# Chunked attention ahead of a two-layer MLP: scores in 64x32 parts and values in 64x64 parts of the PE array

## The chip, the cores and the metric

The kernel runs on one core of one Trainium2 chip. The metric is the device time of one execution in microseconds (us), lower is better. The kernel before takes 1089.06 us, the median of three runs (1088.07 to 1089.83).

## What is computed

Attention over chunks of 32 tokens (4 batches, 8 heads, 768 tokens, head size 64), then two MLP layers. Each chunk sees 8 memory keys, 16 tokens to its left, itself and 8 tokens to its right, 64 keys in all (fewer at the ends of the sequence).

```python
q_c = q[:, :, c_start:c_end]                       # 32 queries
k_full = np.concatenate([mem_k, k_ctx], axis=2)    # 8 + up to 56 keys
v_full = np.concatenate([mem_v, v_ctx], axis=2)
scores = scale * np.matmul(q_c, k_full.transpose(0, 1, 3, 2))
a = np.exp(scores - np.max(scores, axis=-1, keepdims=True))
a = a / (np.sum(a, axis=-1, keepdims=True) + 1e-09)
out[:, :, c_start:c_end] = np.matmul(a, v_full)
...
x = attn_out.transpose(0, 2, 1, 3).reshape(3072, 512)
h = x @ w_in                       # 512 -> 2048
y = softplus(h) @ w_out            # 2048 -> 512
# second layer: the same shapes, with PReLU (alpha per column) for softplus
```

## The kernel before

**Attention** is cut into 24 tiles t of 128 tokens (`QT`); a tile has four chunks and 8 heads in 4 pairs (`NPAIR`). For one tile, in this order:

- SP loads Q in two halves (`load_q`, 64 partitions each), K (`load_k`) and V in six pieces (`load_v`). Loads go through one in-order queue; each waits until the eighth before it has landed. POOL copies the 8 memory keys to both ends of K's runs (`a_mem`, two copies).
- PE computes the scores (`a_scores`). For tiles 0 to 7 that is 32 matmuls on parts of 64 rows by 32 columns of the array: the two heads of a pair (e = 0, 1) lie on the two halves of the rows, and head e of chunk c writes the 32 PSUM partitions c*64 + e*32, so that four different parts are used in turn. For tiles 8 to 23 it is 16 matmuls on 128 rows by 64 columns, with queries that are zero in the other head's places (`q_late`, zeroed once by `others`). The result fills one PSUM bank.
- DVE takes the maximum (`a_max`) and subtracts it (`a_shift`), ACT takes the exponential, DVE sums and inverts, and DVE (POOL for tiles 4 to 7) scales. For tiles 0 to 3 DVE only scales the maximum (`a_bias`), and ACT subtracts and exponentiates in eight pieces.
- PE transposes (`a_transpose`, 4 matmuls), and ACT copies the result to `pt` in four pieces (`a_turned`), into corners of a block form whose other corners are zero (`no_corners`, once).
- PE multiplies by V (`a_values`: 16 matmuls on 128 rows by 64 columns, with 64 columns streamed). ACT writes the high part of x (`a_high`), DVE the low part (`a_low`).

PSUM's eight banks are four for accumulators (`ps_acc`; the first four tiles' scores use them too), two for `ps_h` and two for attention (`ps_a`), which scores, transposes and values take in turn.

**Layer 1** has 96 steps; step i multiplies 512 tokens (block b, four tiles) by one weight column block f. A step is two units of 12 matmuls each: `pe_h` (x times w_in, written `ps_hh` in the profile) and `pe_out` (activation times w_out, `ps_o`). Steps 0 to 3 are block 0 with f = 0 to 3, steps 4 to 7 block 1 with the same weights; so step 4 needs tiles 4 to 7. Each weight half comes as a raw load of 64-bit words (`raw`), which DVE converts with five operations (`word`), ACT rounds to a high part (`wsplit`), and DVE subtracts for a low part. Three raw buffers are in use at a time; the next raw load waits until DVE is done with the one three before. **Layer 2** (`ps_q`) follows.

**The order** of all of this is laid down by a planner (`Plan`, `schedule`): each piece has an engine, an assumed duration, a due time, things it must follow, and rooms that it takes and gives. The table `O` shifts due times by kind of piece. Every engine then runs its pieces strictly in that order, so an operation that waits for a DMA holds all that stands behind it on its engine. Where PE would idle in the first 90 us of the plan, matmuls on zeros fill in (`keep_busy`).

In the rows below all instructions have line L71, since a helper issues them; they are told apart by the names of their tiles: `ps_s` scores, `ps_t` transposes, `ps_x` values, `qk`, `qt`, `kt`, `v` the loaded inputs, `x` the attention's result, `g` the activation.

Of the kernel before, what the change touches and what calls it, by code (L numbers as in the profile page):

```python
# [185 lines left out]
def attention_mlp_mlp_kernel(ctx: ExitStack, tc, qk, v, w1, w2, consts, out):  # L186
# [129 lines left out]
    raw_q, q_t, k_t, v_t, st, s_room = {}, {}, {}, {}, {}, {}  # L316
    pt = [tpool.tile([P, NPAIR, 2, D], F32, tag=tag, name="pt") for tag in ("tb", "tl")]
    both = gpool.tile([P, 2, NPAIR, 2, D], F32, tag="g", name="pt2")
    pt2 = [both[:, u] for u in range(2)]

    def pt_of(t):
        return pt2 if t < TB and t % 2 else pt

    q_late = apool.tile([P, 2, 4 * NPAIR, CHUNK], F32, tag="qt", name="qt", bufs=1)

    def others(q, eng):
# [868 lines left out]
```

## Time and profile before

| | |
|---|---|
| median of three runs | 1089.06 us |
| profiled execution, its own time | 1092.29 us |
| its span (first to last instruction) | 1090.2 us |
| PE busy (matmul) | 97% of the span |
| DVE, ACT, POOL busy | 65%, 51%, 16% |
| mean granted TensorE clock | 0.995 of full speed |

The profile gives for each engine its instructions in order of time with the idle time just before them and what released it, and a chain of work that is followed back from the last instruction. The profiled execution's time is 2.1 us above its span and 3.2 us above the median.

### The profile page before, as it was taken

Reading aid. Unit: us, or ns where it says so; the run is one execution under the profiler, and the core shown is the slowest. Engines: PE = TensorE matmul, PEld = TensorE weight load, DVE = VectorE, ACT = ScalarE, POOL = GpSimd, SP = SyncE. Lnnn points to the kernel's source line nnn. Section 1 sums busy time; section 2 is a strip of 40 time slices with the busy share of each in tenths; the row PEclk is TensorE's granted clock in tenths of the full one; section 3 lists DMA queues with packets and bytes.
Section 4 is the critical chain, followed back from the end, with each engine's and each line's share of the span. In section 5 each row is a group of like instructions: output and inputs, shape, how many; then the busy total and the mean of one; then the engine's idle time right before and its main releaser. Section 6 shows DMA issues by size and latency. Waiting matters only on the chain.

```text
span 1090.2 us, 16860 instructions
## 1 busy us (share of the span) xinstructions
PE 1061.8 (97%) x6241; PEld 872.5 (80%) x6245; DVE 705.3 (65%) x1182; ACT 556.9 (51%) x988; POOL 173.0 (16%) x217
## 2 busy tenths in 40 slices
PE   5789999999999999999999999999999999999998
PEld 3568888878888888888888888888888888888886
DVE  5779978454554454464366256678766779566976
ACT  4564435455544554453244346664455755456643
POOL 1110112422322232224233400000000010000000
PEclk8999999999999999999999999999999999999999
DMA  8966674757554554554365484799875999856904
GB/s 216 203 178 190 192 188 109 180 159 178 152 156 148 167 174 125 184 156 136 106 203 189 161 300 137 274 286 323 199 284 174 322 298 261 242 217 256 373 1 77
DMA packets 173841, 214.56 MB, mean 197 GB/s; under 512 B 96064, under 2 KB 125888, under 8 KB 166848
## 3 DMA queue, kind: packets, MB, share of 16 engines
q1 hardware_dynamic: 169456, 196.59, 56.8%
q0 software_dynamic: 4032, 16.78, 8.2%
q8 instruction: 49, 0.80, 0.3%
q14 instruction: 32, 0.26, 0.1%
q10 hardware_dynamic: 272, 0.13, 0.0%
HBM read 154.74 MB, written 46.14 MB: 184 GB/s over the span
## 4 chain that ended last, share of the span: by engine, by line
PE 92%; DMA 4%; SPq 2%; DVE 2%; issue 0%; ACT 0%; POOL 0%; DVEq 0%; ACTq 0%
PE ps_q L71 42%; PE ps_hh L71 23%; PE ps_o L71 23%; SPq L71 2%; DMA raw<-in_w_dram 2%; PE ps_x L71 2%; PE ps_s L71 2%; DMA v<-in_v_dram 1%; PE ps_t L71 1%; DVE word L71 1%; DMA qk<-in_qk_dram 1%; DVE x L71 0%; DVE wsplit L71 0%; DVE g L71 0%; ACT pt L71 0%
## 5 line engine op out<-in xcount | busy, mean ns | idle before, releaser
L71 PE MATMUL ps_o<-g,wsplit 128*128 128x512 f32 x1152 | 281.2, 393 | 1.3 <-DVE g L71 1.3
L71 PE MATMUL ps_hh<-x,wsplit 128*128 128x512 f32 x1152 | 279.4, 391 | 2.9 <-ACT x L71 1.8
L71 PEld LDWEIGHTS ps_hh<-x,wsplit 128*128 128x128 f32 x1152 | 214.7, 188 | 48.6 <-ACT x L71 2.3
L71 PEld LDWEIGHTS ps_o<-g,wsplit 128*128 128x128 f32 x1152 | 215.8, 189 | 46.6 <-DVE g L71 1.6
L71 PE MATMUL ps_q<-xop,win 128*128 128x512 f32 x1008 | 229.1, 389 | 0.0
L71 PE MATMUL ps_q<-g,wout 128*128 128x512 f32 x1008 | 229.1, 389 | 0.0
L71 PEld LDWEIGHTS ps_q<-xop,win 128*128 128x128 f32 x1008 | 189.2, 188 | 39.3
L71 PEld LDWEIGHTS ps_q<-g,wout 128*128 128x128 f32 x1008 | 189.0, 188 | 39.6 <-DVE g L71 0.2
L71 DVE TENSOR_TENSOR g<-ta,g 128x512 fp32r<-128x512 f32 x96 | 70.4, 733 | 131.1 <-ACT g L71 130.6
L71 ACT CAST g<-gb 128x512 fp32r<-128x512 f32 x168 | 100.9, 622 | 91.1 <-PE ps_q L71 66.1
L71 DVE TENSOR_TENSOR g<-gb,g 128x512 fp32r<-128x512 f32 x168 | 114.2, 687 | 37.0 <-ACT g L71 35.1
L71 ACT CAST g<-ta 128x512 fp32r<-128x512 f32 x96 | 59.6, 621 | 113.9 <-PE ps_o L71 113.7
L71 ACT ACTIVATE ta<-ps_hh 128x512 f32<-128x512 f32 x96 | 57.4, 598 | 108.9 <-PE ps_hh L71 106.6
L71 DVE SCALAR_TENSOR_TENSOR word<-raw,word 128x512 int32<-128x512 int32 x128 | 93.0, 727 | 2.7
L71 ACT ACTIVATE tp<-gb 128x512 f32<-128x512 f32 x48 | 30.4, 633 | 91.5 <-DVE gb L71 91.5
L71 POOL TENSOR_TENSOR wst<-wsum,wst 128x512 fp32r<-128x512 f32 x32 | 42.8, 1338 | 146.9 <-ACT wst L71 146.9
L71 DVE TENSOR_SCALAR word<-raw 128x512 int32<-128x512 int32 x64 | 29.6, 463 | 51.2 <-DMA raw<-in_w_dram 31.7
L71 DVE SCALAR_TENSOR_TENSOR gb<-gb,tp 128x512 f32<-128x512 f32 x48 | 33.2, 692 | 44.0 <-ACT tp L71 44.0
L71 DVE TENSOR_SCALAR word<-word 128x512 f32<-128x512 f32 (+1 forms) x128 | 56.6, 447 | 1.9
L71 ACT ACT_TABLE_LOAD x38 | 48.8, 1283 | 12.0 <-DVE nm L71 11.3
L71 POOL TENSOR_TENSOR wst<-word,wst 128x512 fp32r<-128x512 f32 (+1 forms) x32 | 35.2, 1100 | 119.2 <-ACT wst L71 119.2
L71 POOL DMA_DIRECT2D gb<-gb x12 | 10.3, 862 | 262.7 <-DVE g L71 169.8
(82 smaller groups left out, 879.3 us busy)
## 6 DMA issues: line engine op xcount, KB each, us to landing
wout<-out_ops SPq DMA_DIRECT2D x42, 1024.0 KB
raw<-in_w_dram SPq DMA_DIRECT2D x64, 512.0 KB
win<-in_ops SPq DMA_DIRECT2D x24, 1024.0 KB
win<-in_ops SPq DMA_DIRECT2D x24, 768.0 KB
out_ops<-wst SPq DMA_DIRECT2D x56, 256.0 KB
in_ops<-wst SPq DMA_DIRECT2D x24, 512.0 KB
gb<-gb POOLq DMA_DIRECT2D x12, 1024.0 KB, 13.7
v<-in_v_dram SPq DMA_DIRECT2D x48, 128.0 KB
```

The source lines that it names most:

```text
L71: i = getattr(self.engine, name)(*args, **kw)
```

## The change

Scores of all tiles use 64x32 parts. The head e now chooses the half of the rows and the PSUM bank, and the 32 columns are chosen by chunk and pair, so that eight matmuls in a row go to eight different parts. Scores lie in the first 256 columns of two banks; for tiles 4 to 23 these are the two banks of one fixed tile, `pair_room`, whose second halves take the transposes and the values. Tiles 0 to 3 use the four accumulator banks, two tiles to a bank, and `ps_h` for their transposes. Values use 64x64 parts: 32 matmuls with 32 columns streamed in place of 16 with 64. The block form is gone, so a tile's transposed scores are copied by one ACT operation, nothing is zeroed, and Q of the late tiles is loaded in two pieces, not four. K of tiles 0 to 7 is loaded as one run of 640 numbers a partition; the memory keys aren't copied to its ends, and their scores are matmuls of their own (two for a chunk at either end of a tile, so 48 matmuls, not 32). The maximum and the shift of tiles 0 to 3 come in two pieces. V's six loads have other rows and another order. The planner's rooms, durations and table `O` (70 numbers) are new, so that pieces stand in another order.

```diff
-O = {'km': 86.2, 's': 61.12, 'm': -43.08,
...
+O = {'km': -97.11, 's': 13.09, 'm': 12.26,
...
-    ps_a = ctx.enter_context(room_pool("ps_a", 2, bass.MemoryType.PSUM))
+    ps_pair = early.enter_context(room_pool("ps_pair", 1, bass.MemoryType.PSUM))
...
+    def key_parts(t, j):
+        if t >= 2 * TB:
+            return [(0, KEYS[j], KW)]
+        if j in (1, 2):
+            return [(0, j * CHUNK, KW)]
+        n = KW - NMEM
+        return [(0, MEM0, NMEM), (NMEM, 0, n)] if j == 0 else [(0, KT - n, n), (n, MEM0, NMEM)]
...
     def load_k(t):
-        sp.dma_start(out=k_t[t][:, :, NMEM:NMEM + KT], in_=qk[t][:, QN:].rearrange("p (g k) -> p g k", k=KT))
+        at = 0 if t < 2 * TB else NMEM
+        sp.dma_start(out=k_t[t][:, :, at:at + KT], in_=qk[t][:, QN:].rearrange("p (g k) -> p g k", k=KT))
...
+    pair_room = ps_pair.tile([P, 2, N2], F32, tag="pair", name="ps_a")
...
-            for g in range(NPAIR):
-                for j in range(NC):
-                    u, c = divmod(j, 2)
-                    for e in range(2):
-                        rows, at = slice(e * D, (e + 1) * D), c * D + e * CHUNK
-                        pe.matmul(
-                            ps[at:at + CHUNK, g, u, :], lhsT=q[rows, u * NPAIR + g, c * CHUNK:(c + 1) * CHUNK],
-                            rhs=k_t[t][rows, g, KEYS[j]:KEYS[j] + KW], start=True, stop=True,
-                        )
...
+        for n in range(2):
+            for u in range(2):
+                for c in range(2):
+                    for m in range(2):
+                        for e in range(2):
+                            rows, at, g = slice(e * D, (e + 1) * D), (2 * c + m) * CHUNK, 2 * n + m
+                            j = 2 * u + c
+                            for to, key, many in key_parts(t, j):
+                                pe.matmul(
+                                    banks[e][at:at + CHUNK, n, 1 - u, to:to + many],
+                                    lhsT=q[rows, u * NPAIR + g, c * CHUNK:(c + 1) * CHUNK],
+                                    rhs=k[rows, g, key:key + many], start=True, stop=True,
+                                )
...
-        for u in range(2):
-            for c in range(2):
-                act.copy(
-                    out=pt_of(t)[u][c * D:(c + 1) * D, :, :, c * CHUNK:(c + 1) * CHUNK],
-                    in_=ps[u * D:(u + 1) * D, :, c * D:(c + 1) * D].rearrange("p g (e q) -> p g e q", e=2),
-                )
...
+        act.copy(out=pt[t % 2].rearrange("p (a m) k -> p a (m k)", a=2), in_=turned.pop(t))
...
-        for u in range(2):
-            for g in range(NPAIR):
-                for e in range(2):
-                    d0 = u * DM + (2 * g + e) * D
-                    pe.matmul(
-                        ps[e * D:(e + 1) * D, g, u * D:(u + 1) * D], lhsT=src[:, d0:d0 + D], rhs=pt_of(t)[u][:, g, e, :],
-                        start=True, stop=True,
-                    )
...
+        for g in range(NPAIR):
+            for c in range(2):
+                for u in range(2):
+                    for e in range(2):
+                        keys, d0, q0 = slice((1 - u) * D, (2 - u) * D), (2 * g + e) * D, (2 * c + g % 2) * CHUNK
+                        pe.matmul(
+                            ps[e * D:(e + 1) * D, u, g, c * CHUNK:(c + 1) * CHUNK], lhsT=src[keys, c ^ u, d0:d0 + D],
+                            rhs=pt[t % 2][keys, 2 * e + g // 2, q0:q0 + CHUNK], start=True, stop=True,
+                        )
...
-        add("corners", "DVE", 2.4, 0, no_corners)
-        add("qzero", "POOL", 1.5, 40, lambda: others(q_late, pool))
```

How this moves instructions is seen at three places. The first is SP's queue from the last loads of tile 7 to tile 8's K. In the rows of before `qk_618` and `v_697` are Q, K and V of tile 7 (its first Q half stands further ahead), `raw` is a raw load of weights, `qt` and `kt` are Q and K of tile 8:

```order
L71 DMA qk_618<-in_qk_dram 64x8x64
L71 DMA qk_618<-in_qk_dram 128x4x160
L71 DMA v_697<-in_v_dram 8x512
L71 DMA v_697<-in_v_dram 56x512
L71 DMA v_697<-in_v_dram 64x512 x2
L71 DMA v_697<-in_v_dram 56x512
L71 DMA v_697<-in_v_dram 8x512
L71 DMA raw<-in_w_dram 128x512
L71 DMA qt<-in_qk_dram 64x8x32 x4
L71 DMA kt<-in_qk_dram 128x4x160
```

Now, where `qk_748` and `v_818` are tile 7 and `qk` is tile 8:

```order
L71 DMA qk_748<-in_qk_dram 64x8x64 x2
L71 DMA qk_748<-in_qk_dram 128x640
L71 DMA raw<-in_w_dram 128x512
L71 DMA v_818<-in_v_dram 64x512 x2
L71 DMA v_818<-in_v_dram 56x512 x2
L71 DMA v_818<-in_v_dram 8x512 x2
L71 DMA qk<-in_qk_dram 64x8x64
L71 DMA raw<-in_w_dram 128x512
L71 DMA qk<-in_qk_dram 64x8x64
L71 DMA qk<-in_qk_dram 128x4x160
```

The raw load that stood behind V of tile 7 stands ahead of it. The raw load after that, which came behind all eleven loads of tile 8, comes behind the first of nine.

The second place is PE between the first unit of `pe_out` and the first unit of step 4. In the rows of before `qk_520` and `qk_618` are the scores of tiles 6 and 7 (tile 5's stand two units further ahead), and `v_521`, `v_619`, `v_697` the attention weights of tiles 5, 6 and 7:

```order
L71 MATMUL ps_s<-qk_520 32x64 x32
L71 MATMUL ps_hh<-x,wsplit 128x512 x12
L71 MATMUL ps_s<-qk_618 32x64 x32
L71 MATMUL ps_t<-cst,v_521 128x128 x4
L71 MATMUL ps_o<-g,wsplit 128x512 x12
L71 MATMUL ps_t<-cst,v_619 128x128 x4
L71 MATMUL ps_x<-pt,v_521 64x64 x16
L71 MATMUL ps_hh<-x,wsplit 128x512 x12
L71 MATMUL ps_x<-pt,v_619 64x64 x16
L71 MATMUL ps_t<-cst,v_697 128x128 x4
L71 MATMUL ps_o<-g,wsplit 128x512 x12
L71 MATMUL ps_x<-pt,v_697 64x64 x16
```

Now the scores of tile 5 come first, then one unit of `ps_hh`, the scores of tile 6, one unit of `ps_o` and the scores of tile 7, and behind these (`v_644`, `v_749`, `v_818` are tiles 5, 6 and 7; `zero` rows fill):

```order
L71 MATMUL ps_a<-cst,v_644 128x128 x4
L71 LDWEIGHTS zero
L71 MATMUL ps_a<-zero 128x512
L71 MATMUL ps_a<-pt,v_644 64x32 x32
L71 MATMUL ps_a<-cst,v_749 128x128 x4
L71 MATMUL ps_a<-cst,v_818 128x128 x4
L71 MATMUL ps_a<-pt,v_749 64x32 x32
L71 MATMUL ps_hh<-x,wsplit 128x512 x12
L71 MATMUL ps_a<-pt,v_818 64x32 x32
L71 MATMUL ps_o<-g,wsplit 128x512 x12
L71 MATMUL ps_hh<-x,wsplit 128x512 x12
```

Scores move behind units that stood behind them, and the values of tiles 5 and 6, which had a unit between them, come together.

The third place is DVE at tile 11 (`s_sb` its weights; `x` the low part of tile 10). Before:

```order
L71 MEMSET ps_s 64x4x8
L71 TENSOR_REDUCE nm<-ps_s 128x8
L71 TENSOR_TENSOR s_sb<-ps_s,nm 128x512
L71 TENSOR_SCALAR word<-raw 128x512
L71 TENSOR_TENSOR x<-ps_x,x 128x4x128
L71 TENSOR_SCALAR word<-word 128x512 x2
L71 SCALAR_TENSOR_TENSOR word<-raw,word 128x512 x2
L71 TENSOR_TENSOR g<-ta,g 128x512
L71 TENSOR_REDUCE sm<-s_sb 128x8
```

Now:

```order
L71 MEMSET ps_a 64x2x2x8
L71 TENSOR_REDUCE nm<-ps_a 128x8
L71 TENSOR_TENSOR g<-ta,g 128x512
L71 TENSOR_TENSOR s_sb<-ps_a,nm 128x512
L71 TENSOR_REDUCE sm<-s_sb 128x8
L71 TENSOR_TENSOR x<-ps_a,x 128x4x128
L71 TENSOR_SCALAR sm<-sm 128x8
L71 RECIPROCAL r<-sm 128x8
L71 TENSOR_TENSOR s_sb<-s_sb,r 128x512
L71 TENSOR_SCALAR word<-raw 128x512
```

The first operation on a raw load (`word<-raw`), which waits for its DMA, stood between tile 11's shift and its sum, and stands behind the tile's whole chain.

## Rows read from the trace of the kernel before

**Rows 1.** page: busy time, share of the span and instructions of each engine

```profile
PE 1061.8 (97%) x6241; PEld 872.5 (80%) x6245; DVE 705.3 (65%) x1182; ACT 556.9 (51%) x988; POOL 173.0 (16%) x217
```

**Rows 2.** windows: stretch, its us, busy of PE, PEld, DVE, ACT, POOL, clock, DMA

```profile
30.00:40.00 10.00, 9.14 (x137) 7.06 (x138) 7.40 (x14) 6.82 (x12) 0.43 (x2) 1.00 1.10 243
```

**Rows 3.** the chain in order of time: start, us, what

```profile
25.78 4.25 DMA v<-in_v_dram
...
34.92 8.92 DMA raw<-in_w_dram
...
45.20 6.82 DMA qk<-in_qk_dram
...
66.33 5.12 DMA raw<-in_w_dram
...
633.23 451.63 PE ps_q L71 x1992
```

**Rows 4.** PE's timeline, start: start, us, what [idle before, releaser]

```profile
31.92 1.47 PE L71 MATMUL ps_x<-pt,v 128*64 128x64 f32 x32
...
35.20 5.72 PE L71 MATMUL ps_hh<-x,wsplit 128*128 128x512 f32 x24
...
44.95 4.35 PE L71 MATMUL ps_o<-g,wsplit 128*128 128x512 f32 x11 [1.27 <-DVE g L71]
...
52.80 1.12 PE L71 MATMUL ps_s<-qk 64*32 64x64 f32 x64 [2.42 <-POOL qk L71]
53.85 3.06 PE L71 MATMUL ps_hh<-x,wsplit 128*128 128x512 f32 x12
...
69.07 3.00 PE L71 MATMUL ps_o<-g,wsplit 128*128 128x512 f32 x12
...
77.28 5.51 PE L71 MATMUL ps_hh<-x,wsplit 128*128 128x512 f32 x23 [1.11 <-DVE x L71]
```

**Rows 5.** DVE's timeline, start of the program

```profile
43.87 0.43 DVE L71 TENSOR_SCALAR word<-raw 128x512 int32<-128x512 int32 x1 [2.04 <-DMA raw<-in_w_dram]
...
76.54 0.68 DVE L71 TENSOR_TENSOR x<-ps_x,x 128x512 fp32r<-128x512 f32 x1
77.14 0.42 DVE L71 TENSOR_SCALAR word<-word 128x512 int32<-128x512 int32 x1
77.48 0.42 DVE L71 TENSOR_SCALAR word<-raw 128x512 int32<-128x512 int32 x1
```

**Rows 6.** ACT's timeline, the same stretch

```profile
62.92 1.54 ACT L71 COPY pt<-ps_t 64x256 f32<-64x256 f32 x4
64.48 0.59 ACT L71 CAST x<-ps_x 128x512 fp32r<-128x512 f32 x1
```

**Rows 7.** SP's queue, issue times of loads

```profile
57.14 2.68 SPq L71 DMA_DIRECT2D qt<-in_qk_dram  x4
...
66.33 13.46 SPq L71 DMA_DIRECT2D raw<-in_w_dram  x5
```

**Rows 8.** the chain again, tiles 8, 12: start, us, what

```profile
161.67 1.08 PE ps_s L71 x32
...
176.59 0.44 PE ps_t L71 x4
177.03 2.77 PE ps_o L71 x12
...
237.28 1.08 PE ps_x L71 x32
238.36 0.93 PE ps_s L71 x32
239.29 2.95 PE ps_o L71 x12
```

**Rows 9.** tile 11: DVE's wait, then PE's (timelines)

```profile
227.47 0.43 DVE L71 TENSOR_SCALAR word<-raw 128x512 int32<-128x512 int32 x1 [3.72 <-DMA raw<-in_w_dram]
...
233.92 0.63 PE L71 MATMUL ps_t<-cst,s_sb 128*128 128x128 f32 x4 [2.50 <-DVE s_sb L71]
```

More of the change, by code (lines that the diff above doesn't have):

```diff
@@ L313, in operands_at @@
         return [in_ops[q][:, :, k:k + n, :].rearrange("p a k n -> p a (k n)")]
[L316 to L326, printed above, removed]
-        for e in range(2):
-            half = q[e * D:(e + 1) * D].rearrange("p c (n e) k -> p c n e k", e=2)
-            for c in range(2):
-                eng.memset(half[:, c, :, 1 - e], 0.0)
+    raw_q, k_t, v_t, st, s_room = {}, {}, {}, {}, {}
+    pt = [tpool.tile([P, NPAIR, P], F32, tag=tag, name="pt") for tag in ("tb", "tl")]
     def room_qk(t):
@@ new lines, in score_banks, with score_parts @@
+    def score_banks(t):
+        if t < TB:
+            part = slice(t // 2 * HK, (t // 2 + 1) * HK)
+            return [first_banks[t % 2 * 2 + e][:, part] for e in range(2)]
+        return [pair_room[:, e, :HK] for e in range(2)]
+    def score_parts(t):
+        if t < TB:
+            return [(slice(4 * e, 4 * e + 4), ps.rearrange("p (n k) -> p n k", k=KW)) for e, ps in enumerate(score_banks(t))]
+        return [(slice(0, SLOTS), pair_room[:, :, :HK].rearrange("p e (n k) -> p e n k", k=KW))]
@@ new lines, in a_scores @@
+    def a_scores(t):
+        banks = [ps.rearrange("p (g w k) -> p g w k", w=2, k=KW) for ps in score_banks(t)]
+        keep_busy(("s", t), first_banks[t % 2 * 2] if t < TB else pair_room[:, 0, :])
+        q, k = raw_q[t], k_t[t]
+        for n in range(2):
[11 more added lines that the diff above has]
+                                )
@@ L460, in a_transpose @@
     def a_transpose(t):
-        ps = turned[t] = ps_a.tile([P, NPAIR, P], F32, tag="pa", name="ps_t")
-        keep_busy(("t", t), ps.rearrange("p g k -> p (g k)"))
+        if t < TB:
+            ps = turned[t] = ps_h.tile([P, 2, HK], F32, tag="h", name="ps_t")
+            keep_busy(("t", t), ps.rearrange("p a k -> p (a k)"))
+        else:
+            ps = turned[t] = pair_room[:, :, HK:]
+        for m in range(NPAIR):
+            pe.transpose(ps[:, m // 2, m % 2 * P:(m % 2 + 1) * P], st[t][0][:, m, :], ident)
@@ L838, in second @@
             if q == 0:
[L839 removed]
+                ps = ps_of[ka] = [bank(spaces[ka]) for _ in range(2)] if ka in spaces else ps_of[A11]
             g = g2.pop(n)
@@ L1017, in tile @@
-            add(("km", t), "POOL", 0.36, due - when_due("km"), lambda: a_mem(t), [("qk", t, 2)])
-            after_s = [("km", t)] + queries + ([("s", prev)] if prev >= 0 else []) + ([("t", TB - 1)] if t == TB else []) + ([("pt", prev)] if t > 2 * TB else []) + ([("h", step)] if step else [])
-            if t > 3 * TB:
+            add(("qr", t), "", 0.0, soon, lambda: room_qk(t), free_qk, qrooms)
+            for e in range(2):
+                dma(("q", t, e), 0.66, 0.72, soon, lambda e=e: load_q(t, e), [("i", "q", t, 0) if e else ("qr", t)])
@@ new lines, in tile @@
+            dma(("qk", t, 2), 0.65 if few else 0.4, 1.4 if few else 1.1, soon, lambda: load_k(t), [("i", "q", t, 1)])
+            add(("vr", t), "", 0.0, soon + 2, lambda: room_v(t), [("i", "qk", t, 2)] + ([("i", "v", prev)] if few else []), vrooms)
+            dma(("v", t), 2.9, 1.9, (O["va"], O["vb"], O["vc"], O["vd"])[t] if start else due - 24, lambda: load_v(t), [("vr", t)])
+            if few:
+                add(("km", t), "POOL", 0.36, due - when_due("km"), lambda: a_mem(t), [("qk", t, 2)])
```

192 lines of the change are left out of this document (84 added, 108 removed).

## The prediction

> **What bounds the kernel now.** I read the page first: PE is busy for 97% of the span [rows 1]. The chain in order of time says where the rest lies: from 77.28 on it holds PE's work almost alone, up to the last matmul at 633.23 + 451.63 = 1084.86 [rows 3, 4]. A unit of 12 matmuls takes 451.63 / 1992 x 12 = 2.72 us [rows 3]. So the span of 1090.2 splits into layer 1 (192 units, 522.2), layer 2 (2016 matmuls, 457.1), 5.3 behind the last matmul, and 105.6 that is neither. Layer 2's order is the same row for row on DVE, and its matmuls are the same, so the change can only touch the 105.6.
>
> The 105.6 has two parts. At 77.28 PE had done seven units and one matmul, counted on its timeline from 35.20 to 69.07 [rows 4]; 77.28 - 7 x 2.72 - 0.23 = 58.0 us are lost in the start. The other 47.6 are attention pieces that stand between units, and one stall. In the chain a piece of scores or values alone takes 1.08, scores right behind values 0.93, and the unit behind either takes 2.95 instead of 2.72; a transpose takes 0.44 and 0.05 in the unit behind it [rows 8]. PE's order has four pieces alone, 14 pairs and 16 transposes: 4 x 1.31 + 14 x 2.24 + 16 x 0.49 = 44.4. The stall is 2.50 before tile 11's transpose: it waits for DVE, and DVE for a raw load [rows 9]. That is 46.9 of the 47.6.
>
> **The start, walked through.** From 30 us on the granted clock is 1.00, the level of 2.4 GHz [rows 2]. Durations are those of rows; landings are estimates from the landings there, less what is no longer queued ahead. On DVE a tensor operation starts the next 0.60 later, one with a scalar 0.34 later [rows 5].
>
> First two units. V of tile 1 landed at 25.78 + 4.25 = 30.03, and tile 3's weights went to the same buffer as tile 1's, so their copies came behind tile 1's values; tile 3's values started at 31.92 [rows 3, 4]. Now V of tile 1 is loaded ahead of V of tile 3, and one copy (taken as 0.6, like ACT's cast of the same size [rows 6]) replaces four in 1.54. Tile 3's values start when its V lands, 30.1: 1.8 sooner. Ahead of the units stand tile 4's scores with 48 matmuls in place of 32, 0.5 more (1.05 x 48 / 32 = 1.58, from the 1.05 between scores and unit at 52.80 [rows 4]). The units start at 35.2 - 1.8 + 0.5 = 33.9.
>
> First `ps_o`. It started at 44.95 [rows 4]; the low part of its activation stood on DVE behind the first operation on a raw load, which landed at 34.92 + 8.92 = 43.84 [rows 3, 5]. In SP's new order one K less, 320 KB, is ahead of that load: 1.3 us at the 243 GB/s of that stretch [rows 2]. So 42.5, and with 0.34 and 0.60 the unit starts at 43.5 and ends at 46.2.
>
> Next `ps_hh`. It started at 53.85 because tile 6's scores stand ahead of it and waited for their K, landed at 45.20 + 6.82 = 52.02, and for POOL's copies of the memory keys [rows 3, 4]. Now only tile 5's scores are ahead, whose K has landed: 46.2 + 1.58 = 47.8 to 50.5, six us sooner. Tile 6's K is issued behind a raw load that waits for the landing at 42.5; with the same 6.82 it lands at 49.5, so its scores follow without a wait: 52.1; a unit to 54.8; tile 7's scores to 56.4.
>
> One room. Tiles 5 to 7 now share `pair_room`: a transpose must wait until the values ahead of it are drained. Maximum, shift and exponential of tile 7 (0.60, 0.34 for a raw operation between, 0.60, 0.6) stand ahead of tile 5's copy on ACT, so that copy is done at 59 and tile 5's values at 60.1. Then cast 0.59, low part 0.60, transpose 0.44, copy 0.6, transpose 0.44, copy 0.6, and some 0.1 of hand-over at each: tile 6's values run from 64.0 to 65.1. A unit to 67.8, tile 7's values to 68.9, a unit to 71.6, and there seven units are done. The low part of tile 7, which step 4 needs, is due by 71.2. The raw loads must keep up: the one that landed at 66.33 + 5.12 = 71.45 stood behind 66.33 - 57.14 = 9.2 us of tile 8's loads [rows 3, 7] and comes now behind one of these, near 62.
>
> So step 4 starts at 71.8, where 77.05 (77.28 less one matmul) is its match: **-5.2**, with bounds of -8 (no waits in the one room) and +2 (raw loads land as before, and the rooms add 2).
>
> **Pieces between units.** No row has scores by eight parts or values by 64x64. Scores: the nearest row is the early tiles' 32 matmuls on 64x32 parts, 1.05 [rows 4], though with four parts in turn; below, half of that (0.53); above, twice the late form's 1.08 for twice its matmuls (2.16). Values: the same row has the same number of matmuls and gives 1.05; the ends are 0.53 and 2.16 again. I take 1.05 for both, as each lies nearest to it in number, and 2.10 for a pair, since the two now have different parts and the 0.15 saved by a second piece of the same form has no row to stand on. In the new order there are ten pieces alone, 11 pairs and 16 transposes: 10 x 1.28 + 11 x 2.33 + 16 x 0.49 = 46.3, **+1.9**. The lower ends make it 29.6 (-14.8), the upper ones 81.8 (+37).
>
> **Stall.** At tile 11 no raw operation stands any more between shift and sum, so the 2.50 goes. In its place the one room asks that tile 9's values are drained within one unit before tile 10's transpose: cast, low part and hand-over, 1.4 of 2.72, if neither engine has anything in front. I leave 1.0 for that and its like (0 to 4): **-1.5**.
>
> **At nothing.** The zeroing of corners and of `q_late` ends before anything needs DVE or POOL. The shorter K queue and two Q loads fewer per late tile free SP, which waits rather than works there. ACT's 0.9 a tile behind tile 8 is hidden by units of PE; if the cover went, it would be up to 0.9 x 16. Two smaller maxima for one cost DVE some 0.1 in tiles 0 to 3, inside the first 30 us.
>
> **Sum.** -5.2 + 1.9 - 1.5 = -4.8, so a span of 1085.4 where 1090.2 was. The profiled execution took 1092.29 and the median is 1089.06, so I take the difference to the median: **1084.3**. A measurement tells about 0.2%, 2.2 us, from no change.
>
> **Rivals.**
>
> 1. *A value matmul keeps its price when its columns are halved* (slower). Each of 64 records then costs 0.93 / 32 = 29 ns or more [rows 8]: 1.86 to 2.16 for a tile, 0.8 to 1.1 above my 1.05, 16 times: +13 to +18, or 1097 to 1102. It decides against the change from (4.8 / 16 =) 0.3 more, a piece of 1.35. Against it: the early scores' records cost 1.05 / 64 = 16 ns, so there is no fixed 29. Half-way, at 1.5, the time is 1091.5. Chance 0.14. The Trainium skill's page "TensorEngine Tiling (Array Packing)", section Performance Considerations (Instruction Overhead), gives a matmul about 60 cycles of overhead and warns against tiling a dimension that is already small; by that rule the 32 columns save nothing. No row here has 32 columns, and 16 ns are 39 cycles at 2.4 GHz, below those 60, so the trace so far doesn't bear it out.
> 2. *Eight parts do run at once.* Pieces of 0.53: -14.8 for my +1.9, or 1067.6. For it: eight matmuls in a row on eight parts, in two banks. Against it: the loads of weights are as many as matmuls, and no row shows records closer than those of the early scores. Chance 0.07.
> 3. *The start doesn't shorten.* Raw loads land as now, or tiles 5 to 7 in one room cost what the early units gain: 1084.3 + 5.2 = 1089.5, between 1086.5 and 1092. For it: DVE is held by raw loads, as at 43.87 for 2.04 [rows 5], and each such hold I moved by an estimate. Chance 0.21.
>
> **How the numbers follow.** My forecast has 0.58, from 1079 to 1088.5. The range leaves out rival 2 and the far half of rival 1 (0.07 + 0.09) and little else: 1079 to 1092. Faster (under 1086.9): 0.52 of the forecast, rival 2, 0.03 of rival 3: 0.62. Within 0.2%: 0.06, 0.12 of rival 3, 0.01 of rival 1: 0.19. Slower: 0.13 of rival 1, 0.06 of rival 3: 0.19.
>
> **What would show it.** On PE's timeline: the first `ps_hh` near 34, the first `ps_o` near 43.5, the second `ps_hh` group near 48, and seven units done by 72. In the chain: pieces of 1.05 alone and 2.1 as a pair, the unit behind at 2.95, no stall at tile 11. I am wrong in the walk if a raw load's first operation on DVE holds the low part of x or g beyond these times; in the pieces if a pair is not near 2.1; and on the whole if PE stalls between units after step 4, where I have no wait but those of the one room.

## The result, and the profile of the changed kernel

The change made the kernel slower. Four runs of the changed kernel have a median of 1098.51 us (1096.57 to 1098.75), four of the kernel before 1088.57 (1088.07 to 1089.83): a ratio of 1.0086, 95% interval 1.0068 to 1.0103. The prediction was 1084.3, in a range of 1079 to 1092, so it missed by 14.2 us and on the wrong side. The profiled execution of the changed kernel took 1098.33, its span 1096.6.

The page's line of busy times answers to [rows 1]; PE has 1535 more instructions and is busy for 7.4 us more.

```profile
PE 1069.2 (98%) x7776; PEld 875.6 (80%) x7781; DVE 707.6 (65%) x1179; ACT 534.6 (49%) x916; POOL 165.2 (15%) x197
```

The windows (stretch, its us, busy us of PE, PEld, DVE, ACT, POOL, granted clock, DMA share, GB/s) hold the first surprise. [Rows 2] had a clock of 1.00 in 30:40; now it reads 0.50, the level of 1.2 GHz, and it is low again in 60:80 and in 620:640.

```profile
30.00:40.00 10.00, 7.61 (x204) 5.59 (x204) 5.05 (x10) 2.99 (x5) 0.00 (x0) 0.50 0.98 258
...
60.00:70.00 10.00, 5.76 (x176) 4.23 (x174) 7.89 (x19) 4.02 (x8) 3.83 (x5) 0.87 0.66 192
70.00:80.00 10.00, 8.73 (x145) 7.07 (x146) 7.30 (x14) 3.98 (x7) 0.00 (x0) 0.62 0.31 107
...
90.00:620.00 530.00, 530.00 (x4263) 435.67 (x4262) 310.98 (x528) 231.80 (x369) 139.73 (x164) 1.00 0.53 160
620.00:640.00 20.00, 16.48 (x68) 13.29 (x68) 5.63 (x11) 5.50 (x10) 9.85 (x10) 0.94 0.42 147
```

PE's timeline in the start answers to [rows 4]. From tile 4 on all attention pieces write `ps_a` (before that scores write `ps_s` and transposes `ps_t`), so they are told apart by form: 64*32 is scores, `cst` transposes, 64*64 values, `zero` fill. A drain of values is ACT's cast and DVE's subtraction (DVE x), which read them out of PSUM.

```profile
19.39 0.79 PE L71 MATMUL ps_s<-qk 64*32 64x8 f32 x54 [1.21 <-issue]
...
34.49 1.93 PE L71 MATMUL ps_a<-pt,v 64*64 64x32 f32 x64
37.85 0.59 PE L71 MATMUL ps_a<-zero 128*128 128x512 bf16 x1 [1.43 <-DVE x L71]
38.79 1.69 PE L71 MATMUL ps_a<-qk 64*32 64x8 f32 x96 [0.36 <-issue]
40.42 7.22 PE L71 MATMUL ps_hh<-x,wsplit 128*128 128x512 f32 x24
...
64.42 0.63 PE L71 MATMUL ps_a<-cst,v 128*128 128x128 f32 x4 [1.81 <-DVE v L71]
...
66.02 1.14 PE L71 MATMUL ps_a<-pt,v 64*64 64x32 f32 x64
68.68 1.09 PE L71 MATMUL ps_a<-cst,v 128*128 128x128 f32 x4 [1.52 <-DVE x L71]
70.53 1.09 PE L71 MATMUL ps_a<-cst,v 128*128 128x128 f32 x4 [0.77 <-ACT pt L71]
72.35 1.93 PE L71 MATMUL ps_a<-pt,v 64*64 64x32 f32 x64 [0.73 <-ACT pt L71]
74.22 4.63 PE L71 MATMUL ps_hh<-x,wsplit 128*128 128x512 f32 x12
78.78 1.13 PE L71 MATMUL ps_a<-pt,v 64*64 64x32 f32 x64
...
82.71 2.88 PE L71 MATMUL ps_hh<-x,wsplit 128*128 128x512 f32 x12
```

The first `ps_hh` comes at 40.4, where it came at 35.2 and was forecast at 33.9. The scores of tile 4 and the zero ahead of them, which stand before it, wait for the last drain of tile 3's values (DVE x). The chain of tiles 5 to 7 (from 64.42) first waits 1.81 for tile 5's attention weights (DVE v), then 0.7 to 1.5 for a drain or a copy ahead of each further step up to tile 6's values. Tile 6's values take 1.93 and the transposes of tiles 6 and 7 take 1.09 each, where others of the same form take 1.14 and 0.6 at a clock of 1.00. Tile 5's values (66.02) take 1.14, those of tile 7 (78.78) 1.13. The fifth `ps_hh` piece, with which step 4 starts, comes at 82.71.

In the chain (start, us, what) step 4 starts at 82.88. Pieces between units answer to [rows 8], and tile 11's transpose at 239.36, without a gap ahead of it, to the stall in [rows 9]; `ps_a` x53 is scores (some records are missing), x64 values, x117 a pair.

```profile
82.88 2.72 PE ps_hh L71 x12
...
172.63 0.79 PE ps_a L71 x53
173.42 2.99 PE ps_hh L71 x12
...
232.62 1.06 PE ps_a L71 x64
233.68 2.95 PE ps_hh L71 x12
236.63 2.73 PE ps_o L71 x12
239.36 0.44 PE ps_a L71 x4
...
259.01 1.85 PE ps_a L71 x117
```

The same view where layer 1 ends (in [rows 3], layer 2 went on from 633.23 without a gap):

```profile
633.06 3.50 DMA out_ops<-wst
...
636.64 0.62 ACT wst L71
637.26 0.49 ACT tc L71
...
637.79 453.43 PE ps_q L71 x1992
```

and PE's timeline there:

```profile
625.95 5.60 PE L71 MATMUL ps_q<-xop,win 128*128 128x512 f32 x24
...
637.79 22.59 PE L71 MATMUL ps_q<-xop,win 128*128 128x512 f32 x92 [3.52 <-ACT tc L71]
```

Layer 2's weight operands (`wst`) were prepared so late that the last two casts of them waited on ACT for a store to free their buffer, and the copy `tc` of layer 2's first product stood behind them. Before, ACT's last two casts of `wst` came 13 us earlier, ahead of layer 2's first product on PE:

```profile
622.96 1.14 ACT L71 CAST wst<-wsum 128x512 fp32r<-128x512 f32 x2
...
624.90 5.60 PE L71 MATMUL ps_q<-xop,win 128*128 128x512 f32 x24
```

Now PE had nothing to do for 3.52 us, and the 92 matmuls behind it took 22.59 where 92 x 451.63 / 1992 = 20.86 is usual [rows 3]: 1.7 more.

**Where the time came from.** Step 4 starts at 82.88 in the chain instead of 77.05: +5.8. From there to layer 2's first product (timeline, 625.95 against 624.90) 4.8 were gained. The gap between the layers lost 3.5, and layer 2 took 453.43 instead of 451.63, +1.8. That is +6.3 of a span that grew by 6.4. The medians differ by 3.5 more, mainly since the profiled execution of before was 3.7 above its median and that of after at its median. These traces don't show where a typical execution of before is shorter, so a share of the losses may be missing from this sum.

### The profile page after: what moved, and what is told of

Read it like the earlier page. It is cut to its first block, busy times and chain, and to the rows that moved or that the text cites. A ratio compares the mean times of both kernels' runs of the same rounds, so it can differ in the third digit from the quotient of the medians.

```text
span 1096.6 us, 19710 instructions
## 1 busy us (share of the span) xinstructions
PE 1069.2 (98%) x7776; PEld 875.6 (80%) x7781; DVE 707.6 (65%) x1179; ACT 534.6 (49%) x916; POOL 165.2 (15%) x197
## 4 chain that ended last, share of the span: by engine, by line
PE 94%; DMA 2%; SPq 2%; issue 1%; POOL 1%; ACT 1%; DVE 0%; POOLq 0%; ACTq 0%
PE ps_q L71 41%; PE ps_hh L71 24%; PE ps_o L71 24%; PE ps_a L71 5%; SPq L71 2%; DMA qk<-in_qk_dram 1%; DMA raw<-in_w_dram 1%; DMA out_ops<-wst 0%; POOL wst L71 0%; DMA in_ops<-wst 0%; POOL wsum L71 0%; DMA v<-in_v_dram 0%; ACT pt L71 0%; DVE x L71 0%; ACT x L71 0%
## 5 line engine op out<-in xcount | busy, mean ns | idle before, releaser
L71 PEld LDWEIGHTS ps_hh<-x,wsplit 128*128 128x128 f32 x1152 | 217.1, 190 | 45.5
L71 DVE TENSOR_TENSOR g<-ta,g 128x512 fp32r<-128x512 f32 x96 | 77.0, 802 | 164.3 <-ACT g L71 163.8
L71 POOL TENSOR_TENSOR wst<-wsum,wst 128x512 fp32r<-128x512 f32 x32 | 44.4, 1389 | 152.1 <-ACT wst L71 142.9
L71 DVE TENSOR_SCALAR word<-word 128x512 int32<-128x512 int32 (+1 forms) x128 | 56.5, 446 | 2.2
L71 ACT ACT_TABLE_LOAD x38 | 48.8, 1283 | 11.2 <-DVE nm L71 10.6
L71 PEld LDWEIGHTS ps_a<-pt,v 64*64 64x64 f32 x1536 | 26.9, 145 | 12.1 <-issue 6.4
```

The lines of the kernel that those rows point to most:

```text
L71: i = getattr(self.engine, name)(*args, **kw)
```

## Experiments

Every kernel is the changed one with the edit shown. Times are medians; a difference is to the 1098.5 of the changed kernel, and ratios are to the kernel before, run alongside. That kernel's median was 1088.6 beside the changed one and 1087.0 to 1088.6 beside the others, so a difference of medians can be off by 1.6; "by the ratios" compares with the 1.0086 of the changed kernel instead, which is fairer. The places in a timeline come from one execution each. The theories at the start were: **the clock** (zeros wait in the same room as the piece behind them, PE stands still and its clock falls), **the room** (values, drains and the next piece take turns in one pair of banks), **K in short matmuls**, and **the weights of layer 2** for the second loss.

**e3_w2: layer 2's weights 6 us earlier.**

```diff
-k, due = halves[j], when[24 + 64 * j // (4 * NQ)]
+k, due = halves[j], when[24 + 64 * j // (4 * NQ)] - 6
```

> The changed kernel with the loads, conversions, sums and stores of the second layer's weights due 6 us earlier, nothing else. Theory A (TensorE's 3.52 us without work ahead of the second layer come from two wst casts of ScalarE that wait for the store of an earlier wst and stand ahead of the copy tc): the idle time before the ps_q at 637.79 is gone (under 0.3), the last copies of wst lie before the last ps_hh of the first layer, the window behind it shows a granted clock of 1.00, and the time is 3.5 to 5.3 us shorter, 1093.2 to 1095. Theory B (the copy tc would wait for something else anyway, or the weights that come earlier delay the first layer's ends by as much): 1097.5 to 1099.

Measured: 1092.7, or 5.8 less; ratio 1.0046 (1.0031 to 1.0061). PE's timeline has no idle time there, and the 115 matmuls take 26.23, the usual 0.228 each:

```profile
634.13 26.23 PE L71 MATMUL ps_q<-xop,win 128*128 128x512 f32 x115
```

So theory A holds: the gap and the slow matmuls behind it are one cause, worth 5.3 in the traces, 5.8 in the medians and 4.4 by the ratios.

**e1_fill: zeros into half of the pair, and ahead of more pieces.**

```diff
-        for _ in range(spare.pop(name, 0)):
-            pe.matmul(ps, lhsT=zero, rhs=zero[:, :1].to_broadcast([P, N2]), start=True, stop=True)
+        for _ in range(2 * spare.pop(name, 0)):
+            pe.matmul(pair_room[:, 0, :HK], lhsT=zero, rhs=zero[:, :1].to_broadcast([P, HK]), start=True, stop=True)
...
+        keep_busy(("t", t))
```

> The changed kernel with one thing altered: the zeros that fill TensorE's planned gaps go to the first half of the pair of banks, in 256 columns and twice as many, and no longer to the bank that the next piece writes; the gaps planned ahead of the transposes of tiles 5 to 7, which got none, get theirs too. Theory A (the start is lost because the zeros wait for the same room as the piece behind them, so that TensorE stands still and its granted clock falls): the window 30:40 rises from a granted clock of 0.50 to 0.85 or more and 70:80 from 0.62 to 0.85 or more, the first ps_hh comes at 36 to 38 instead of 40.5, the scores of tile 4 no longer stand 1.43 us behind the reading of tile 3's values, the fourth ps_hh piece at about 70 instead of 74.3; 1092 to 1095.5 us instead of 1098.5. Theory B (one room of values, x then its two drains then the next x, and the later V, set the start whatever the clock): the clock may rise, the first ps_hh stays at 39 or later, 1097 to 1099.

Measured: 1104.7, or 6.2 more; ratio 1.0156 (1.0116 to 1.0195). Neither theory had that. The zeros didn't come ahead of the wait, as they were meant to:

```profile
33.82 1.44 PE L71 MATMUL ps_a<-zero 128*128 128x256 bf16 x6 [1.43 <-DVE x L71]
```

The zeros write the first half of the bank, the drain they wait for reads the second: the kernel orders accesses to PSUM by bank, not by address. So the zeros still ran behind the wait. The Trainium skill's page "PSUM — Partial Sum Buffer", section "PSUM bank collisions raise a hardware error", states such a rule: PSUM has to be guarded by bank and quadrant, not by address. This row and the zero at 37.85 in the changed kernel agree with it.

That isn't where most of the time went, though. In this trace the first `ps_hh` comes at 44.88, 4.5 later than in the changed kernel. Of this, 4.0 were lost by the end of tile 0's values: the first scores start 0.9 later (8.61), and PE stops twice with nothing to wait for that the trace shows, where the changed kernel stopped once (1.21 at 19.39).

```profile
19.71 1.21 PE L71 MATMUL ps_s<-qk 64*32 64x64 f32 x69 [2.19 <-issue]
...
24.80 0.43 PE L71 MATMUL ps_a<-pt,v 64*64 64x32 f32 x6 [2.04 <-issue]
```

So this run says what is waited for, but not what zeros cost.

**e4_nofill: no zeros at all** (the `for` over zeros runs 0 times).

> The changed kernel without any zeros in TensorE's gaps (the output is the same). Theory A (clock): the granted clock is low in more of the first 80 us than now, also in 10:30, and the first ps_hh comes at 41.5 or later; 1100 to 1106 us. Theory B (the zeros do no good and hold the scores of tiles 2 and 4 back, since they write a bank that is still read): the first ps_hh comes at 39 or earlier, 1095 to 1098.

Measured: 1096.6, or 1.9 less, theory B's range, with the first `ps_hh` at 38.06; ratio 1.0079 (1.0054 to 1.0104), which the noise doesn't tell from the changed kernel's. The scores of tile 2 come 2.6 us earlier than behind their zeros (15.51). PE ran at the low level's durations until inside the first `ps_hh` group:

```profile
28.55 1.93 PE L71 MATMUL ps_a<-pt,v 64*64 64x32 f32 x64 [1.40 <-DVE x L71]
...
38.06 8.02 PE L71 MATMUL ps_hh<-x,wsplit 128*128 128x512 f32 x24
```

So the clock by itself is not the cause of the first half of the start loss: a start that runs at the lower level throughout, and is rid of the zeros, is no later. (The column of the granted clock reads 1.00 up to 60 in this trace, beside durations that are double; here only the durations tell the level.)

**e6_bank: the same zeros in banks that nobody else holds.**

```diff
+if name in (("s", 0), ("s", 2)):
+    ps = pair_room[:, 0, :]
+elif name[0] != "h" and name[1] <= TB:
+    ps = first_banks[0]
```

> The changed kernel with the zeros of the first 40 us in banks that nothing else holds at their time (the pair of banks ahead of the scores of tiles 0 and 2, the first bank of the old scores after that); count and order unchanged. In e1_fill the zeros still waited for the last reader of the pair, since a bank, not a half of it, is what is waited for; and without any zeros (e4_nofill) the time was 1.9 us shorter. Theory A (zeros that run inside the waits keep the clock up and stand no longer between a wait and the piece behind it): the granted clock of 20:40 rises to 0.85 or more, the values of tiles 1 and 3 take 1.1 to 1.2 us instead of 1.93, the first ps_hh comes at 36 to 38, 1093 to 1096 us. Theory B (too few zeros: the clock stays low as it does without them): first ps_hh at 38 to 40, 1096 to 1098.5.

Measured: 1096.7 (1092.5 to 1098.9), or 1.9 less, at the edge of the two ranges; ratio 1.0069 (1.0041 to 1.0097). The profiled execution, the fastest of six, had its first `ps_hh` at 36.78 and a granted clock of 1.00 in 30:40, as theory A has it, but its scores of tile 4 waited 2.04 for a load of `qk`. The spread is wide, and whether better placed zeros would win back a part of the first half stays open.

**e7_room: values of tiles 1 and 3 in the banks of the first scores.**

```diff
-        room = pair_room[:, :, HK:]
-        keep_busy(("v*", t), pair_room[:, 0, :])
+        if t in (1, 3):
+            banks = first_banks[t - 1:t + 1]
+        else:
+            banks = [pair_room[:, u, :] for u in range(2)]
+        keep_busy(("v*", t), banks[0])
...
-                            ps[e * D:(e + 1) * D, u, g, c * CHUNK:(c + 1) * CHUNK], lhsT=src[keys, c ^ u, d0:d0 + D],
+                            ps[u][e * D:(e + 1) * D, g, c * CHUNK:(c + 1) * CHUNK], lhsT=src[keys, c ^ u, d0:d0 + D],
```

> The changed kernel with the values of tiles 1 and 3 in the banks of the first scores, which are free by then, and not in the pair (each is drained by two instructions an engine for it, one a bank); order and zeros unchanged. Theory A (the single pair serialises the first tiles: values, both drains, next values, and the scores of tile 4 behind the last drain): the scores of tile 4 follow the values of tile 3 at once, the first ps_hh comes 2 to 4 us earlier, at 36.5 to 38.5, 1094.5 to 1097 us. Theory B (V lands too late for that, 28.8 us for tile 1 and 33.3 us for tile 3, and the ps_hh needs the drains of tile 3 anyway): first ps_hh at 39.3 or later, 1097.5 to 1099.

Measured: 1094.4, or 4.2 less; ratio 1.0059 (1.0037 to 1.0081), so 2.9 less by the ratios, with intervals that overlap a little. Scores of tile 4 no longer wait for a drain:

```profile
33.25 0.70 PE L71 MATMUL ps_a<-qk 64*32 64x8 f32 x43
34.53 0.79 PE L71 MATMUL ps_a<-qk 64*32 64x8 f32 x53 [0.57 <-issue]
35.24 6.14 PE L71 MATMUL ps_hh<-x,wsplit 128*128 128x512 f32 x24
```

The first `ps_hh` comes 5.2 us earlier, the first `ps_o` at 44.36, the second `ps_hh` group at 48.53, the end of tile 7's scores at 56.8: within 1.4 us of the forecast walk (33.9, 43.5, 47.8, 56.4). The zeros ahead of these values went to the other banks too, and the clock in 30:40 was 1.00, so this run alone doesn't part the room from the zeros. e14 below does: neither it nor e4 has zeros, both run these values at the low level (1.93 to 2.1), and up to the first `ps_hh` e7's edit is the difference between them. Tile 1's values start at 25.8 (the row below the table) instead of 28.55, without e4's wait of 1.40, and the first `ps_hh` at 33.71 instead of 38.06. So the one room in tiles 0 to 4 is the first half of the start loss. From there on the walk fails again: fifth `ps_hh` piece at 77.2, not 71.8.

**e9_h3: the fourth `ps_hh` piece ahead of tile 5's transposes.**

```diff
+move(("wh", 6), ("m", 7))
+move(("wl", 6), ("m", 7))
+move(("h", 3), ("t", 5))
```

> The changed kernel with one unit moved: the low half of its weights (wl of the seventh weight tile, VectorE) and the copy that it needs (wh, ScalarE) stand ahead of the maximum of tile 7's scores, and the fourth ps_hh piece stands ahead of the transposes of tile 5 instead of behind the values of tile 6. Theory A (the second half of the start loss is the chain of tiles 5 to 7 in one room, 61.4 to 74.2 us, that no ps_hh covers, and in which the granted clock falls to 0.50): the 1.81 us ahead of the transposes of tile 5 are covered, the values of tiles 5 and 6 take 1.1 to 1.3 us instead of 1.93 for tile 6, the fifth ps_hh piece starts 3 to 5 us earlier than 82.7, and the time is 1093.5 to 1096 us instead of 1098.5. Theory B (the chain of VectorE and ScalarE between the tiles sets the end, whatever TensorE does meanwhile): the fifth ps_hh piece at 81 or later, 1097 to 1099.

Measured: 1098.1, no change (0.4 less; ratio 1.0098, 1.0082 to 1.0115). The wait of 1.81 was covered and the clock in 60:70 was 1.00, yet the fifth `ps_hh` piece came at 82.22. The values of tile 7 now stand at the end of the same chain:

```profile
72.94 1.94 PE L71 MATMUL ps_a<-pt,v 64*64 64x32 f32 x64 [0.73 <-ACT pt L71]
76.30 1.93 PE L71 MATMUL ps_a<-pt,v 64*64 64x32 f32 x64 [1.43 <-DVE x L71]
```

Theory B. The unit that covered 1.81 in one place no longer covers the 1.43 ahead of tile 7's values, and tile 7's values and the `ps_o` behind them (4.21) now run at a low clock too (0.53 in 70:80). Moving one unit doesn't help; the chain itself must be shorter.

**e12_th: transposes of tiles 4 to 7 in the `ps_h` banks.**

```diff
-if t < TB:
+if t < 2 * TB:
     ps = turned[t] = ps_h.tile([P, 2, HK], F32, tag="h", name="ps_t")
```

> The changed kernel with the transposes of tiles 4 to 7 in the ps_h banks, as those of tiles 0 to 3, so that the pair of banks holds only scores and values there (with them come the 3 planned zeros ahead of each of the three transposes). Theory A (one room for transposes and values makes the chain of tiles 5 to 7): the transposes of tiles 6 and 7 follow the values of tile 5 at once (1.52 and 0.77 us of idle time gone, and 0.73 ahead of the values of tile 6), the fifth ps_hh piece starts 2 to 4 us earlier than 82.7, 1094.5 to 1096.5 us instead of 1098.5. Theory B (the chain is that of the drains x, high half, low half, next x, and the transposes only stand in its shadow): the fifth ps_hh piece at 81.5 or later, 1097.3 to 1099.

Measured: 1093.2, or 5.3 less; ratio 1.0049 (1.003 to 1.0068), so 4.0 less by the ratios.

```profile
67.72 0.82 PE L71 MATMUL ps_t<-zero 128*128 128x512 bf16 x3
68.38 0.60 PE L71 MATMUL ps_t<-cst,v 128*128 128x128 f32 x4
70.15 0.65 PE L71 MATMUL ps_t<-cst,v 128*128 128x128 f32 x4 [1.18 <-POOL v L71]
70.74 1.14 PE L71 MATMUL ps_a<-pt,v 64*64 64x32 f32 x64
...
78.87 3.02 PE L71 MATMUL ps_hh<-x,wsplit 128*128 128x512 f32 x12
```

Although this execution's first `ps_hh` was late (42.39), its fifth is at 78.87, 3.8 earlier than in the changed kernel. The durations here are those of a granted clock of 1.00 again. So theory A: one room for transposes and values makes the second half of the start loss. The zeros that came with the edit have a part in the clock: e11 and e13 below differ by the same edit without any zeros, and there the fifth `ps_hh` comes 5.2 earlier and the time is 2.7 less, though the clock stays low (0.77 in 60:70 of e13, 0.89 in 70:80). So the room counts by itself, and that the low clock follows from the room's waits alone isn't shown.

**e15_two: e3_w2 and e12_th together, nothing else.**

> The changed kernel with only two edits: the second layer's weights due 6 us earlier (e3_w2) and the transposes of tiles 4 to 7 in the ps_h banks (e12_th). If the two causes are apart, as their places in the trace say (625 to 640 us and 60 to 83 us): 1098.5 - 5.8 - 5.3 = 1087.4 us, 1086.4 to 1088.6, the time of the kernel before (1087 to 1089), the fifth ps_hh piece at 78 to 79.5 and no idle time between the layers. If they share a part (for instance because a shift of the whole first layer changes how the weights' stores meet the copies tc): 1089 to 1092.

Measured: 1087.5 (1085.5 to 1088.9), ratio 1.0006 (0.9997 to 1.0015), so the causes add up: 1098.5 - 5.8 - 5.3 = 1087.4, and by the ratios 1.0086 - 0.0040 - 0.0037 = 1.0009. PE's timeline, start and end of layer 1:

```profile
77.07 2.88 PE L71 MATMUL ps_hh<-x,wsplit 128*128 128x512 f32 x12
...
628.34 21.92 PE L71 MATMUL ps_q<-xop,win 128*128 128x512 f32 x96
```

Step 4 starts where it did before the change, at 77.1, and nothing is lost at the transition. Layer 2 then starts 4.7 earlier than in the trace of before (628.34 against 633.06), while the medians agree: the trace of before lies 3.7 above its median, and where the other executions are shorter isn't shown.

**K as before: e2_kback and e5_k2.**

```diff
 def key_run(t):
-    return KT if t < 2 * TB else KN
+    return KN
```

with `a_mem` for all tiles; e2 issues the copies with the load of K, e5 when K has landed by the plan.

> The changed kernel with K of the first eight tiles as before: keys in a run that has a place for the memory keys at both ends, GpSimd copies them there, and each score part is one matmul of 64 columns (128 of them a tile instead of 192). The order of everything else is the changed one. If this part of the change gave what was expected of it (the copies gone from the path to the first scores, about 0.6 us of them a tile in the trace of before), the first scores come 0.5 to 1 us later and the time is 0.3 to 1.5 us longer, 1099 to 1100. If it is a part of what was lost (three matmuls instead of two a pair of parts), the time is 0.5 to 2 shorter.

> K of the first eight tiles as before, once more, with GpSimd's copies of the memory columns set into its queue where each K lands, so that no share of a tile waits behind the copy of a later K (which cost 8.63 us ahead of the transposes of tile 4 in e2_kback); all else as changed. Theory A (the 96 short matmuls a tile, in place of 64 of 64 columns, cost TensorE more than the copies: in the changed kernel the scores of tile 3 stop 1.21 us in the middle with nothing to wait for, in e2_kback they don't, and the first ps_hh came at 36.8 there instead of 40.5): first ps_hh at 36.5 to 38.5, 1093 to 1096.5 us instead of 1098.5. Theory B (the gain of e2_kback at the first ps_hh was of another kind, the clock, and the copies are worth keeping away): first ps_hh at 39.5 or later, 1098 to 1100.

Measured: 1105.8 and 1097.3. The first says little on K: POOL's share of tile 4 stood behind the copy of a later K, and PE waited for it.

```profile
52.40 1.12 PE L71 MATMUL ps_a<-cst,v 128*128 128x128 f32 x4 [8.63 <-POOL v L71]
```

The second gives 1.2 less, between its two ranges, and nothing by its ratio of 1.0085 (1.0058 to 1.0112), with the first `ps_hh` at 39.51. The stop of 1.21 in tile 3's scores (19.39 above) is gone in both, and the values of tile 0 come at 17.7 and 18.7 instead of 20.1, but most of that is lost again in the room behind. K's new form was no gain where it was put, and no large loss.

**All together.** e8_all has K as before, zeros in free banks, e7's room and e3's weights; e10 adds e9's move; e11 is e10 without zeros; e13 adds e12's transposes to e11; e14 is e13 with the changed K.

> The four edits together: K of the first eight as before, zeros in free banks, values of tiles 1 and 3 in the first banks, second layer's weights 6 us earlier. If what each gives adds up: first ps_hh at 34 to 36, no idle time between the layers, 1084 to 1089 us, that is the time of before (1087 to 1089) or a little less. If the gaps of the start are one and the same (all end in the wait for V of tile 3 or in the chain of tiles 5 to 7, which none of the four touches): 1089 to 1091.

> The four edits of e8_all and the moved unit of e9_h3. If the moved unit adds to them: the fifth ps_hh piece at 75 to 77 instead of 79.8 in e8_all, 1084.5 to 1087.5 us, below the kernel before (1087 to 1089). If the two halves of the start hide each other: 1088 to 1090.

> As e10_all_h3, but without any zeros (and so without the edit of their banks). Theory A (zeros that run inside the waits hold the clock up and are worth their place): 1 to 4 us longer than e10_all_h3. Theory B (as in e4_nofill, which was 1.9 us shorter than the changed kernel, the start is better without them): equal to e10_all_h3 or up to 2 us shorter.

> e11_all_h3_nofill (K as before, no zeros, values of tiles 1 and 3 in the first banks, earlier weights of the second layer, moved unit) and the transposes of tiles 4 to 7 in the ps_h banks. If the chain of tiles 5 to 7 in one room is the rest of the loss: the fifth ps_hh piece at 74 to 76 instead of 78.2, 1085 to 1087 us, below the kernel before. If not: 1087.5 to 1089.

> As e13_k2_th, but with the changed K (one run a partition, memory keys' scores apart) in the first eight tiles. In e11_all_h3_nofill the scores of tile 4 wait 1.74 us for GpSimd's copy of the memory keys of K, in e7_room, with the changed K, they don't. If that wait is on the path to the first ps_hh: the first ps_hh 1 to 1.5 us earlier than in e13_k2_th and the time 0.5 to 1.5 us shorter, 1084 to 1086. If the short matmuls' stops of 1 to 2 us in the scores of tile 3 take that back: equal to e13_k2_th within 0.5.

| kernel | median, us | ratio to before (95%) | first `ps_hh` | fifth `ps_hh` piece |
|---|---|---|---|---|
| e8_all | 1089.75 | 1.0016 (1.0002 to 1.003) | 35.66 | 79.82 |
| e10_all_h3 | 1089.27 | 1.0017 (1.0009 to 1.0026) | 37.03 | 77.42 |
| e11_all_h3_nofill | 1088.43 | 1.0004 (0.9992 to 1.0015) | 35.99 | 78.22 |
| e13_k2_th | 1085.70 | 0.9981 (0.9967 to 0.9994) | 35.11 | 73.06 |
| e14_k1_th | 1084.44 | 0.9973 (0.996 to 0.9986) | 33.71 | 74.08 |

e8 and e10 gave less than they were meant to and fell in the second of their two ranges; the chain of tiles 5 to 7 was still whole. Taking the zeros out cost nothing (e11 is 0.8 below e10). With the transposes out of the pair (e13) 2.7 more came, and with the changed K (e14) the first `ps_hh` is 1.4 earlier and the time 1.3 less, but the fifth comes 1.0 later and the two intervals overlap: whether K's new form is worth its short matmuls once nothing behind it waits for a room isn't shown. Both are below the kernel before. In e14 tile 1's values stand right behind the piece ahead of them, and the first `ps_hh` is at 33.71, forecast 33.9:

```profile
25.83 2.00 PE L71 MATMUL ps_s<-pt,v 64*64 64x32 f32 x62
...
33.71 6.48 PE L71 MATMUL ps_hh<-x,wsplit 128*128 128x512 f32 x24
...
74.08 2.88 PE L71 MATMUL ps_hh<-x,wsplit 128*128 128x512 f32 x12
```

## Why the prediction was wrong, step by step

- **The start, walked through (-5.2, measured +5.8): the step that failed.** "Tile 3's values start when its V lands" and "ahead of the units stand tile 4's scores" took no room into account. I counted the one room from tile 5 on, under "One room", though the same `pair_room` holds the values of tiles 0 to 3 and tile 4's scores. Scores and values use different halves of it, and the walk treats that as two rooms; it is one, since a bank is what is waited for (e1). At the first `ps_hh` the walk was off by 6.5 (40.4 for 33.9). With two of these values elsewhere (e7) 5.2 of it went, and my milestones up to tile 7's scores came true within 1.4 us. The raw loads, which I took for the risk, don't appear among DVE's waits from 40 to 83 us.
- **"One room" for tiles 5 to 7** was the right mechanism, mis-sized. From the end of tile 5's values to step 4 I gave it 71.8 - 60.1 = 11.7; it took 82.88 - 67.16 = 15.7 (the end is 66.02 + 1.14). Of the 4.0 more, 3.6 are durations at the low level, or partly at it: 0.8 on tile 6's values (1.93 - 1.14), 0.5 on each of two transposes, 1.8 on a `ps_hh` piece (4.56 - 2.72). The other 0.4 is in the hand-overs, for which I had 0.1 a step. The room itself, its waits included, the walk had nearly right; e12 shows what leaving it gives.
- **"From 30 us on the granted clock is 1.00"** was read from one stretch of before, 30:40 [rows 2], in which PE hardly waited. The next stretch of the same trace doesn't bear it out:

  ```profile
  40.00:50.00 10.00, 7.89 (x111) 5.87 (x111) 7.51 (x19) 5.12 (x9) 1.67 (x3) 0.83 0.86 203
  ```

  In the changed kernel the low clock cost 3.6 in the chain of tiles 5 to 7, by the sum just made. In the first 40 us e4, at the low level and without zeros, was no later.
- **Pieces between units (+1.9, measured about -1.9).** A piece of scores takes 0.79 with 0.27 in the unit behind it, values 1.06 and 0.23, a pair 1.85 and 0.24 (unit 2.96): 5 x 1.06 + 5 x 1.29 + 11 x 2.09 + 16 x 0.49 = 42.6 against 44.4 before. That lies inside my bounds, but the value taken was too dear by 0.26 a piece of scores.
- **Stall (-1.5, measured -2.5).** Gone, and no other came: PE is busy for 530.00 of 530.00 in 90:620. Pieces and stall make 4.4 of the 4.8 that were gained there; 0.4 is not accounted for.
- **"The change can only touch the 105.6"** was the second failed step. Layer 2's order was compared on DVE, not at its border: the new table shifts the preparation of layer 2's weights on POOL, ACT and SP, and the in-order queue of ACT carries that into layer 2's first copy. It cost 3.5 + 1.8 in the traces; e3 gives 5.8 by the medians, 4.4 by the ratios.
- **The offset to the median.** I put the profiled execution of before 3.2 above its median and carried that over. The one of after lies at its median. The span was missed by 1096.6 - 1085.4 = 11.2, so 3.0 of the 14.2 come from the offset and from no term of the sum; no run shows what made that execution of before longer. The 11.2 are 11.0 in the start and 5.3 at the border of the layers, less 3.8 in the pieces, 1.0 in the stall and what isn't accounted for.
- **Rivals.** Rival 3 had the right place and too small a price (1092 at most). Rival 1 (values keep their price at half the columns) fell: 64 records of 32 columns take 1.06, that is 17 ns each. The rule from the Trainium skill that I set beside it ("TensorEngine Tiling (Array Packing)", section Performance Considerations, Instruction Overhead: about 60 cycles a matmul) doesn't hold for these records: 17 ns are 40 cycles at 2.4 GHz, and the scores' records, up to 64 columns on eight parts, take 0.79 / 64 = 12 ns, or 30. Rival 2 (half of 1.05) fell too.

**Left open.** What stops PE for 1.0 to 2.4 us in the middle of tile 3's scores when they are 96 short records (1.21 here, 2.38 in e9), and not when they are 64; the trace shows nothing that it waits for. How the typical execution of before runs its start, since the one traced was 3.7 us above the median. Whether the zeros are worth anything in this start (e4 and e11 were no longer without them; e12 had more of them and gained, and e13 gained by the same edit with none).

## What to carry to other kernels

When a change cuts the number of rooms that pieces take turns in, walk every piece that uses the room, from the first one on, with its drain in between; two halves of a PSUM bank are one room. An order table that is retuned for one place moves work everywhere: look at each engine's queue where one phase hands over to the next, not only at the places that the change names. And what fills an engine's waits must not wait for the same thing as the work behind it, or it adds to the wait: in the changed kernel the wait ahead of tile 4's scores ends at 37.85, and the zero puts them at 38.79.

## What the runs showed of the hardware

- Small matmuls on different parts of the array come closer here than in any row shown of before: 12 ns a record for scores in eight parts and two banks (0.79 for 64), where the same count on four parts and one bank took 1.05 [rows 4]. Parts and banks were changed together, so which of them did it is open.
- A low granted clock need not cost time where PE waits for other engines: without zeros (e4) the start ran at the lower level's durations until past 38 us, and the kernel was no longer for it (ratio 1.0079 against 1.0086). In the chain of tiles 5 to 7, where PE's own work is on the path, it cost 3.6 us.
- PE lost clock after a gap of a few microseconds far from the start as well: 620:640, with the 3.52 us at the border of the layers, reads 0.94, and the 92 matmuls behind the gap took 1.7 us more than usual.
